# Taking A's last two wo rows out of the even DMA spread in a two-head decode kernel

## The chip, the cores and the metric

The kernel runs on one core of one Trainium2 chip. Times are device microseconds (us) of that core, one number for each execution; "median" is the median over the executions of one kernel.

In the trace of this kernel TensorE runs the matmuls (2148 of them), VectorE and ScalarE the elementwise work, copies and reductions (146 and 133 instructions), SyncE issues the large DMAs, and each of these has 16 landings, which are read here as those of 16 DMA engines. The program keeps the results of its matmuls in PSUM and places them by partition (row) and bank. The granted clock is the share of its full speed at which TensorE was allowed to run, as the clock's records of a profile give it; its mean over the span is 0.69 in the kernel before.

## The reference

Two attention decodes of one token, A and B, each end in a product with a [4096, 512] matrix `wo`. Only that last product matters here.

```python
def _A_ref(x, k_cache, v_cache, wq, wo):          # B is the same over the last 4096 keys
    q = (x @ wq).reshape(1, 1, 32, 128) ...       # 32 heads of 128
    scores = einsum("bhqd,bhkd->bhqk", q, k) * (128 ** -0.5)   # k, v: 16384 keys for A
    p = softmax(scores); o = einsum("bhqk,bhkd->bhqd", p, v)
    return o.reshape(1, 1, 4096) @ wo             # wo: [4096, 512], bf16, 4 MB
return concatenate([a, b], axis=-1)               # [1, 1, 1024]
```

## The kernel before

The kernel streams 352 MB, nearly all of it K and V, through one DMA queue, in program order, and loads the two `wo` matrices (4 MB each) at the end of the same queue. A `wo` row block of 32 rows lies on each of 128 partitions, so a product with `wo` is 32 matmuls of a one-column weight, 128 deep. A's piece is loaded as 16 and 16 rows a partition, B's as 16, 8, 4, 2 and 2.

```python
def _load_wo(nc, cx, st, j0, n):                       # one piece: n rows a partition
    ...
    src = st.wo.rearrange("(p j) f -> p j f", j=J)     # J = 32
    cx.o(nc.sync.dma_start(out=st.wo_t[:, j0:j0+n, :], in_=src[:, j0:j0+n, :]))

def _fin_rows(nc, cx, sts):                            # attention results -> columns
    for st in sts:                                     # sums of the softmax weights
        cx.o(nc.tensor.matmul(cx.f_ps[st.f_at:st.f_at+H, DH:DH+1], lhsT=cx.cs[:, st.f_at:st.f_at+H], ...))
    ...                                                # recip, orow, then 4 matmuls each into oc_ps

def _out(nc, cx, st, j0, n):                           # multiply one piece
    if j0 == 0:
        st.oc = ...; cx.o(nc.vector.tensor_copy(st.oc[:, :], st.oc_ps[:, 0:J]))
    if cx.out_ps is None:
        cx.out_ps = cx.red_pool.tile([P, 2, 512], F32, tag="red", name="out_ps")
    w = st.DN // st.cols
    out = [cx.out_ps[r:r+1, b, 0:w] for r, b in st.out_at]
    for j in range(j0, j0 + n):
        for x in range(st.cols):
            cx.o(nc.tensor.matmul(out[x], lhsT=st.oc[:, j:j+1], rhs=st.wo_t[:, j, x*w:(x+1)*w],
                                  start=(j == 0), stop=(j == J-1)))
    if j0 + n == J:
        row = ...; cx.o(nc.vector.tensor_copy(row[0:1, 0:w], out[0]))        # "rowA", "rowB"
        if st.cols == 2: cx.o(nc.scalar.copy(row[0:1, w:], out[1]))
        cx.o(nc.sync.dma_start(out=cx.out[...], in_=row[0:1, :]))

# st.out_at: (partition, PSUM bank) of the result
st.out_at = ((0, 0),) if name == "A" else ((64, 0), (96, 1))   # B in two halves of 256 columns
...
pieces = [(stA, 0, J//2), (stA, J//2, J//2)]           # loads, and later multiplications, in this order
j0 = 0
for x in (J//2, J//4, J//8, J//16, J//16):
    pieces.append((stB, j0, x)); j0 += x
...
_fin_rows(nc, cx, (stA, stB))
for p in pieces:
    _out(nc, cx, *p)
```

A's result and the first half of B's lie in the same PSUM bank, number 0, on different partitions.

The softmax here doesn't subtract the row's maximum and nothing guards it: scores larger than these inputs give would overflow.

## Time and profile before

| | before |
|---|---|
| time, median of the 3 runs first given | 823.26 us |
| traffic | 352.6 MB at 429 GB/s |
| busy: VectorE, TensorE | 73%, 37% |
| last B `wo` piece landed | 818.16 us |
| B's last matmul ended | 818.59 us |
| span of the profile | 821.2 us |

Times within a profile count from the first instruction. The first lines are the page of the kernel before: busy time by engine; the DMA engines' busy tenths in 40 slices of the span; the packets; and the queue that fetches instructions.

```profile
PE 301.1 (37%) x2148; PEld 117.3 (14%) x2148; DVE 600.7 (73%) x146; ACT 35.1 (4%) x133; POOL 1.3 (0%) x9
...
DMA  9999999999999999999999999999999999999997
...
DMA packets 8235, 352.62 MB, mean 429 GB/s; under 512 B 916, under 2 KB 920, under 8 KB 1304
...
q8 instruction: 16, 0.26, 0.1%
```

The DMA digit is 9 in every slice but the last: until the tail there is nothing to gain but bytes. The chain of waits of the kernel before (start, duration, what the span was waiting for) ends so:

```profile
756.43 32.55 DMA vt<-in_B_v_cache_dram
788.99 0.02 issue
789.00 29.16 DMA wo_t<-in_B_wo_dram
818.16 0.04 issue
818.21 0.43 PE out_ps L307 x4
818.63 0.41 DVE rowB L316
```

The last DMA engine to finish sets the end. After it come four matmuls, a copy and a store. The timeline of TensorE in the kernel before (start, duration, operation, and in brackets the idle time before it with what ended it):

```profile
803.73 8.75 PE L307 MATMUL out_ps<-wo_t,ocA 128*1 128x512 bf16 x32 [0.25 <-DVE ocA L300]
813.35 1.91 PE L307 MATMUL out_ps<-wo_t,ocB 128*1 128x256 bf16 x32 [0.87 <-DVE ocB L300]
815.69 1.04 PE L307 MATMUL out_ps<-wo_t,ocB 128*1 128x256 bf16 x16 [0.43 <-DMA wo_t<-in_B_wo_dram]
816.91 1.00 PE L307 MATMUL out_ps<-wo_t,ocB 128*1 128x256 bf16 x12 [0.18 <-DMA wo_t<-in_B_wo_dram]
818.21 0.38 PE L307 MATMUL out_ps<-wo_t,ocB 128*1 128x256 bf16 x4 [0.29 <-DMA wo_t<-in_B_wo_dram]
```

In B's phase TensorE waits for data three times, 0.9 us in all (0.43, 0.18 and 0.29). That is all the slack it has: delay it by more and TensorE sets the end, not the DMA.

The opportunity that the change aims at is in the per-engine completions. The trace has 16 updates of the semaphore of a DMA that is spread over all engines, each taken here as one engine's share landing. For the last B piece before, in us:

```
814.96 815.09 815.11 815.21 815.31 815.47 815.65 815.92 | 817.77 817.88 817.92 817.98 817.99 818.10 818.10 818.16
```

Eight engines are done 1.85 us or more before the other eight (815.92 to 817.77); first to last is 3.20 us. In the windows view of the kernel before, the last 5 us that matter (length; busy us of TensorE, its weight loads, VectorE, ScalarE, GpSimd; granted clock; DMA share; GB/s) have the DMA engines busy for 28%:

```profile
core 0: us, PE busy (x) PEld busy (x) DVE busy (x) ACT busy (x) POOL busy (x), PEclk, DMA share, GB/s
...
815.00:820.00 5.00, 2.67 (x38) 1.36 (x32) 0.42 (x1) 0.37 (x1) 0.00 (x0) 1.00 0.28 109
```

### The profile page before, as it was taken

The numbers are of one execution on the slowest core, as the hardware profiler recorded it, in microseconds if no ns is written. First come the engines' busy times: TensorE is split into PE (matmuls) and PEld (weight loads), VectorE is DVE, ScalarE is ACT, GpSimd is POOL, SyncE is SP. The second block draws the span as 40 slices with busy tenths as digits, with TensorE's granted clock in tenths as the row PEclk, the third lists the DMA queues.
The fourth block names the chain that finished last, engine by engine and source line by source line (L and its number), as shares of the span: only waits on it lengthen the run. The fifth ranks groups of instructions, "written<-read, shape, count | busy, mean of one in ns | idle before, by whom it ended". The sixth has DMA issues, their size and how long they took to land.

```text
span 821.2 us, 4767 instructions
## 1 busy us (share of the span) xinstructions
PE 301.1 (37%) x2148; PEld 117.3 (14%) x2148; DVE 600.7 (73%) x146; ACT 35.1 (4%) x133; POOL 1.3 (0%) x9
## 2 busy tenths in 40 slices
PE   3433705143223415060606151423414250606076
PEld 1111202011011102020202020101101020202033
DVE  2099895997496867799196949599659677689921
ACT  0100000000010000000001000000001000000010
POOL 0000000000000000000000000000000000000000
PEclk9855668586767677675858585857666676768599
DMA  9999999999999999999999999999999999999997
GB/s 383 434 457 412 456 412 454 412 454 418 427 442 444 425 441 429 441 416 447 421 445 437 431 435 434 432 423 443 441 418 451 425 445 421 448 413 455 413 424 317
DMA packets 8235, 352.62 MB, mean 429 GB/s; under 512 B 916, under 2 KB 920, under 8 KB 1304
## 3 DMA queue, kind: packets, MB, share of 16 engines
q1 hardware_dynamic: 8212, 352.33, 99.3%
q8 instruction: 16, 0.26, 0.1%
q14 instruction: 3, 0.02, 0.0%
q10 hardware_dynamic: 4, 0.00, 0.0%
HBM read 352.32 MB, written 0.00 MB: 429 GB/s over the span
## 4 chain that ended last, share of the span: by engine, by line
DMA 61%; issue 15%; DVE 13%; PE 11%; ACT 0%; SPq 0%; DVEq 0%
DMA kt<-in_A_k_cache_dram 42%; DMA vt<-in_A_v_cache_dram 12%; PE red L190 7%; DVE kt L178 6%; DVE kt L169 4%; PE acc L231 4%; DMA vt<-in_B_v_cache_dram 4%; DMA wo_t<-in_B_wo_dram 4%; DVE sc L206 2%; ACT p_sb L212 0%; SPq L115 0%; PE out_ps L307 0%; DVE rowB L316 0%; DVEq L169 0%
## 5 line engine op out<-in xcount | busy, mean ns | idle before, releaser
L169 DVE TENSOR_TENSOR kt<-kt,qallA 128x32768 bf16<-128x32768 bf16 (+2 forms) x20 | 276.2, 13810 | 162.5 <-DMA kt<-in_A_k_cache_dram 162.5
L231 PE MATMUL acc<-vt,p_sb 128*8 128x512 bf16 (+1 forms) x1280 | 113.0, 530 | 444.4 <-ACT p_sb L212 344.4
L178 DVE TENSOR_TENSOR kt<-kt 128x16384 bf16<-128x16384 bf16 (+2 forms) x24 | 174.3, 7261 | 0.2
L190 PE MATMUL red<-kt,ident 128*128 128x512 bf16 x640 | 151.2, 396 | 54.6 <-DVE kt L178 54.6
L231 PEld LDWEIGHTS <-p_sb 128*8 128x8 bf16 (+1 forms) x1280 | 37.6, 112 | 515.7 <-ACT p_sb L212 419.8
L190 PEld LDWEIGHTS <-ident 128*128 128x128 bf16 x640 | 63.0, 101 | 142.2 <-issue 47.1
L169 DVE TENSOR_TENSOR kt<-kt,qallB 128x16384 bf16<-128x16384 bf16 x8 | 69.5, 8686 | 2.9 <-DMA kt<-in_B_k_cache_dram 2.9
L206 DVE TENSOR_REDUCE sc<-red 128x256 f32<-128x2048 f32 x20 | 45.7, 2284 | 5.6 <-PE red L190 5.6
L212 ACT ACTIVATE p_sb<-sc,offA 128x256 bf16<-128x256 f32 x32 | 16.0, 500 | 574.7 <-DVE sc L206 574.7
L245 DVE TENSOR_TENSOR acc<-acc,maskA 128x512 f32<-128x512 f32 x16 | 11.1, 694 | 21.4 <-PE acc L231 21.4
L212 ACT ACTIVATE p_sb<-sc,offB 128x128 bf16<-128x128 f32 x32 | 12.4, 388 | 161.2 <-DVE sc L206 161.2
L130 PE MATMUL q_ps<-wq_t,scr 128*128 128x512 bf16 x64 | 15.7, 407 | 6.9 <-DMA wq_t<-in_A_wq_dram 4.9
L251 DVE TENSOR_REDUCE s<-acc 128x128 f32<-128x512 f32 x24 | 16.6, 691 | 0.8
L307 PE MATMUL out_ps<-wo_t,ocA 128*1 128x512 bf16 x32 | 8.8, 443 | 0.3 <-DVE ocA L300 0.3
L245 DVE TENSOR_TENSOR acc<-acc,maskB 128x512 f32<-128x512 f32 x8 | 5.5, 692 | 4.5 <-PE acc L231 4.5
L130 PEld LDWEIGHTS <-scr 128*128 128x128 bf16 x64 | 6.5, 103 | 15.6 <-issue 8.0
L316 DVE CAST rowA<-out_ps 1x512 bf16<-1x512 f32 x1 | 0.7, 678 | 8.8 <-PE out_ps L307 8.8
L259 PE MATMUL f_ps<-s,selA 128*32 128x128 f32 x32 | 6.5, 285 | 0.0
L212 ACT ACTIVATION_READ_ACCUMULATOR p_sb<-sc,offA 128x1 f32 x32 | 6.0, 187 | 0.0
L212 ACT ACTIVATION_READ_ACCUMULATOR p_sb<-sc,offB 128x1 f32 x32 | 6.0, 186 | 0.0
L307 PE MATMUL out_ps<-wo_t,ocB 128*1 128x256 bf16 x64 | 4.3, 272 | 1.8 <-DMA wo_t<-in_B_wo_dram 0.9
L102 DVE CAST scr<-xT 128x128 bf16<-128x128 f32 (+1 forms) x6 | 2.1, 459 | 3.6 <-PE xT L94 3.5
(43 smaller groups left out, 26.4 us busy)
## 6 DMA issues: line engine op xcount, KB each, us to landing
kt<-in_B_k_cache_dram SPq DMA_DIRECT2D x8, 4096.0 KB, 32.4
vt<-in_B_v_cache_dram SPq DMA_DIRECT2D x8, 4096.0 KB, 23.8
wq_t<-in_A_wq_dram SPq DMA_DIRECT2D x1, 4096.0 KB, 12.2
wq_t<-in_B_wq_dram SPq DMA_DIRECT2D x1, 4096.0 KB
wo_t<-in_A_wo_dram SPq DMA_DIRECT2D x2, 2048.0 KB, 22.6
wo_t<-in_B_wo_dram SPq DMA_DIRECT2D x1, 2048.0 KB, 27.0
wo_t<-in_B_wo_dram SPq DMA_DIRECT2D x1, 1024.0 KB, 29.0
wo_t<-in_B_wo_dram SPq DMA_DIRECT2D x1, 512.0 KB
```

Of the source, the lines that this page charges most:

```text
L102: cx.o(nc.vector.tensor_copy(st.xb[:, :, g, :].rearrange("p c (i r) -> p r c i", r=R)[:, g, :, :], xT[:, :].rearrange("p (c o) -> p c o", ...
L130: cx.o(nc.tensor.matmul(q_ps[:, j, :], lhsT=st.xb[:, c, g, :], rhs=w[:, g, j * (512 // DH) : (j + 1) * (512 // DH), :], start=(g == 0 and ...
L169: cx.o(nc.vector.tensor_tensor(out=k, in0=k, in1=q.rearrange("p (o d) -> p o d", o=1).broadcast_to([P, b - a, DH]), op=ALU.mult,))
L178: cx.o(nc.vector.tensor_tensor(out=k[:, :, 0 : DH // 2], in0=k[:, :, 0 : DH // 2], in1=k[:, :, DH // 2 : DH], op=ALU.add,))
L190: cx.o(nc.tensor.matmul(load.red[:, k : k + n, :], lhsT=cx.ident[:, :], rhs=load.kt[:, k : k + n, b * W : (b + 1) * W], start=(b == 0), st ...
L206: cx.o(nc.vector.tensor_reduce(out=sc[:, :], in_=load.red[:, :, :], axis=AX.X, op=ALU.add))
L212: cx.o(nc.scalar.activation(out=u.p[:, :, g, :], in_=sc[:, u.k0 : u.k0 + n].rearrange("p (t e) -> p t e", e=4), func=ACT.Exp, scale=SCALE, ...
L231: cx.o(nc.tensor.matmul(u.acc[r : r + 4 * R, :], lhsT=u.p[:, t, :, :], rhs=u.load.vt[:, k : k + 4, :], start=(t < 4), stop=(t >= T - 4),))
L245: cx.o(nc.vector.tensor_tensor(out=acc, in0=acc, in1=st.mask[:, :].rearrange("p (x o) -> p x o", o=1).broadcast_to([P, 4, DH]), op=ALU.mult,))
L251: cx.o(nc.vector.tensor_reduce(out=u.s[:, :], in_=acc.rearrange("p x d -> p d x"), axis=AX.X, op=ALU.add,))
L259: cx.o(nc.tensor.matmul(cx.f_ps[st.f_at : st.f_at + 32, 0:DH], lhsT=st.sel[:, at : at + 32], rhs=u.s[:, :], start=(u.i == 0), stop=(u.i == ...
L307: cx.o(nc.tensor.matmul(out[x], lhsT=st.oc[:, j : j + 1], rhs=st.wo_t[:, j, x * w : (x + 1) * w], start=(j == 0), stop=(j == J - 1),))
```

## The change

The intent: give bytes of the late engines to the early ones. A's last two rows of each partition (256 KB, 16 KB an engine) are no longer spread over 16 engines. They go into a tile of their own, `wo_x`, by eight DMAs whose slowest dimension is 5 or 3. They are meant to run on only 5 or 3 engines. Four of 5 blocks are queued behind A's `wo` and four of 3 blocks behind B's first 16 rows. Heads 0 to 19 land on partitions 0 to 19, heads 20 to 31 on 32 to 43, so these rows are multiplied 44 deep, by eight matmuls whose weights (`oc_x`) a small "spread" matmul puts in place. Along with it, the two sums of the softmax weights become one matmul, the copies `ocA` and `ocB` both come ahead of A's matmuls, and B's last piece of two rows is cut into two of one row.

```diff
+APART = 2
...
+def _load_apart(nc, cx, st, part):
+    J = st.wo.shape[0] // P
+    H = st.wo.shape[0] // DH
+    n = DH // J
+    if part == 0:
+        cx.wo_x = cx.kt_pool.tile([P, n, APART, st.DN], BF16, tag="kt", name="wo_x")
+        cx.o(nc.gpsimd.memset(cx.wo_x[0:32], 0.0))
+    src = st.wo.rearrange("(h r j) f -> h r j f", h=H, j=J)
+    h0, to, k = ((0, 0, 5), (20, 32, 3))[part]
+    for a in range(4):
+        cx.o(nc.sync.dma_start(
+            out=cx.wo_x[to + a : to + a + 4 * k - 3 : 4],
+            in_=src[h0 + a : h0 + a + 4 * k - 3 : 4, :, J - APART : J, :],
+        ))
...
-    for st in sts:
-        cx.o(nc.tensor.matmul(
-            cx.f_ps[st.f_at : st.f_at + H, DH : DH + 1],
-            lhsT=cx.cs[:, st.f_at : st.f_at + H], rhs=cx.ones_col[:, 0:1],
+    cx.o(nc.tensor.matmul(
+        cx.f_ps[0 : 2 * H, DH : DH + 1], lhsT=cx.cs[:, :], rhs=cx.ones_col[:, 0:1],
...
+    cx.out_ps = cx.red_pool.tile([P, 3, 512], F32, tag="red", name="out_ps")
...
+            cx.o(nc.tensor.matmul(moved, lhsT=cx.spread[:, :], rhs=orow[...][:, :, J - st.apart : J], ...))
+            st.oc_x = cx.small.tile([64, n * st.apart], BF16, tag="oc_x", name="oc_x")
+            cx.o(nc.vector.tensor_copy(st.oc_x[:, :], moved))
...
+        st.oc = cx.singles.tile([P, J], BF16, tag=f"oc{st.name}", name=f"oc{st.name}")
+        cx.o(nc.vector.tensor_copy(st.oc[:, :], st.oc_ps[:, 0:J]))
...
+    todo = [(st.oc[:, j : j + 1], st.wo_t[:, j, :]) for j in range(j0, j0 + n)]
+    last = j0 + n == J - st.apart
+    if st.apart and last:
+        todo += [
+            (st.oc_x[0:44, i : i + 1], cx.wo_x[0:44, i // st.apart, i % st.apart, :])
+            for i in range(DH // J * st.apart)
+        ]
...
-    pieces = [(stA, 0, J // 2), (stA, J // 2, J // 2)]
+    pieces = [(stA, 0, J // 2), (stA, J // 2, J // 2 - APART)]
-    for x in (J // 2, J // 4, J // 8, J // 16, J // 16):
+    for x in (J // 2, J // 4, J // 8, J // 16, J // 32, J // 32):
...
+        if i in (1, 2):
+            ld.add("kt" if i == 1 else None, lambda i=i: _load_apart(nc, cx, stA, i - 1))
```

More of the change, by code (lines that the diff above doesn't have):

```diff
@@ L268, in _fin_rows @@
     H = 32
-    for st in sts:
-        cx.o(nc.tensor.matmul(
-            cx.f_ps[st.f_at : st.f_at + H, DH : DH + 1],
-            lhsT=cx.cs[:, st.f_at : st.f_at + H], rhs=cx.ones_col[:, 0:1],
-            start=False, stop=True, skip_group_check=True,
-        ))
+    cx.o(nc.tensor.matmul(
+        cx.f_ps[0 : 2 * H, DH : DH + 1], lhsT=cx.cs[:, :], rhs=cx.ones_col[:, 0:1],
+        start=False, stop=True, skip_group_check=True,
+    ))
     recip = cx.small.tile([2 * H, 1], F32, tag="recip", name="recip")
@@ L284, in _fin_rows @@
         h = st.f_at
+        if st.apart:
+            moved = cx.out_ps[0:64, 2, 0 : n * st.apart]
+            cx.o(nc.tensor.matmul(
+                moved, lhsT=cx.spread[:, :],
+                rhs=orow[h : h + H, :].rearrange("p (r j) -> p r j", j=J)[:, :, J - st.apart : J],
+                start=True, stop=True, skip_group_check=True,
+            ))
+            st.oc_x = cx.small.tile([64, n * st.apart], BF16, tag="oc_x", name="oc_x")
+            cx.o(nc.vector.tensor_copy(st.oc_x[:, :], moved))
         for r in range(n):
@@ L293, in _fin_rows @@
             ))
+        st.oc = cx.singles.tile([P, J], BF16, tag=f"oc{st.name}", name=f"oc{st.name}")
+        cx.o(nc.vector.tensor_copy(st.oc[:, :], st.oc_ps[:, 0:J]))
 def _out(nc, cx, st, j0, n):
     J = st.wo.shape[0] // P
-    if j0 == 0:
-        st.oc = cx.singles.tile([P, J], BF16, tag=f"oc{st.name}", name=f"oc{st.name}")
-        cx.o(nc.vector.tensor_copy(st.oc[:, :], st.oc_ps[:, 0:J]))
-    if cx.out_ps is None:
-        cx.out_ps = cx.red_pool.tile([P, 2, 512], F32, tag="red", name="out_ps")
     w = st.DN // st.cols
     out = [cx.out_ps[r : r + 1, b, 0:w] for r, b in st.out_at]
-    for j in range(j0, j0 + n):
+    todo = [(st.oc[:, j : j + 1], st.wo_t[:, j, :]) for j in range(j0, j0 + n)]
[5 more added lines that the diff above has]
+        ]
+    for i, (oc, wo) in enumerate(todo):
         for x in range(st.cols):
             cx.o(nc.tensor.matmul(
-                out[x],
-                lhsT=st.oc[:, j : j + 1],
-                rhs=st.wo_t[:, j, x * w : (x + 1) * w],
-                start=(j == 0),
-                stop=(j == J - 1),
+                out[x], lhsT=oc, rhs=wo[:, x * w : (x + 1) * w],
+                start=(j0 == 0 and i == 0), stop=(last and i == len(todo) - 1),
             ))
-    if j0 + n == J:
+    if last:
         row = cx.accs_pool.tile([1, st.DN], BF16, tag="accs", name=f"row{st.name}")
@@ L375, in problem @@
         st.cols = len(st.out_at)
+        st.apart = APART if name == "A" else 0
         st.f_at = 0 if name == "A" else 32
@@ L444 @@
     )
+    cx.spread = cx.singles.tile([32, 64], BF16, tag="spread", name="spread")
+    nc.vector.memset(cx.spread[:, :], 0.0)
+    nc.vector.tensor_copy(cx.spread[:, 0:20], cx.ident[0:32, 0:20])
+    nc.vector.tensor_copy(cx.spread[:, 32:44], cx.ident[0:32, 20:32])
     cx.cs = cx.singles.tile([P, 64], F32, tag="cs", name="cs")
@@ L485 @@
     stB.oc_ps = cx.acc[1]
-    cx.out_ps = None
     _spread_x(nc, cx, stA, 0, 0)
```

## The prediction

> **What bounds it now.** The page gives 352.6 MB at 429 GB/s and a DMA digit of 9 in every slice but the last; VectorE is busy 73%, TensorE 37%. The chain of waits is 61% DMA, and its last 29.2 us are one wait for B's wo, up to 818.2 us; then 0.4 us of matmuls, a 0.4 us copy and the store, to 821.2. So the last DMA engine sets the end.
>
> The engines do not finish together. In the trace's semaphore increments, every late transfer lands in two groups of eight: the last one (256 KB) at 815.0 to 815.9 us on eight engines and at 817.8 to 818.1 on the others. The skew grows over the run: the queue table's 16 instruction packets of 16 KB each delay an engine by about 1.2 us, and eight engines get two each.
>
> **What the change does.** A's last two rows a partition (256 KB) leave the even spread: 16 KB less an engine. A 256 KB piece takes 0.61 us in the tail (2 KB packets of 80 ns), so each engine ends 0.6 us sooner. The same bytes return in DMAs whose outer dimension is 5 or 3. [...] B's last pieces of one row use 1 KB packets (46 ns, as for xrow): +0.1 us.
>
> Eight more issues of about 0.43 us wait for a GpSimd memset (estimated 3.5 us from the smaller memsets, done near 796) and for reused semaphores, some until A's wo lands (803.5 and 808.4); over 2 MB is queued then, so no late engine starves. TensorE: 38 matmuls of 512 columns for A instead of 32, +6 x 0.21 = 1.3 us, starting after the second wo_x group lands (about 812.2). It gets back the 0.9 us gap between A and B (both copies now come first). A ends near 813.6 and B's 3.9 us of matmuls near 817.7: the chain still ends on B's wo. The added setup hides behind the first K load (42 us).
>
> **Predicted: 822.6 us** (-0.65), range 821.8 to 824.3. Faster by over 2%: 0.3%; within 2%: 98.7%; slower by over 2%: 1%.
>
> **What would show it.** Last B landing at 817.5 instead of 818.1; spread of the last landings 1 us or less instead of 3.1; wo_x landings with 11 or 13 early increments and 5 or 3 late ones; B's last matmul right after its load; DMA share of 815 to 820 us above 0.28.
>
> **What would make it wrong.** [...] If wo_x's second group lands late, B's matmuls pile up behind it (+1 us). If small-k issues take longer, B's last pieces start late. A half-speed clock stretch (now 804.7 to 808.1) shifting onto B's matmuls costs 1 to 2 us.

The sum came to 822.6 us, 0.65 below the 823.26 first measured. Terms are cut from it where marked: which engines take the small DMAs, what these engines gain and where they end, and the risk that one of them is late. The 0.6 us that each engine ends sooner puts the late eight at 817.5.

Measured numbers, from the trace of the kernel before: the spread of a DMA's landings grows from 0.46 us for the first K load to 3.20 us; an instruction fetch took 0.88 to 1.0 us; the late eight land on average 2.65 us behind the early eight, which is 1.3 us for each of two fetches where the prediction has 1.2; successive 256 KB pieces land 0.62 to 0.67 us apart on an engine; a 2 KB packet took 84 ns, where the prediction has 80, and a 1 KB one 46. The GpSimd memset took 3.50 us in the trace after.

## The result, and the profile after

The changed kernel took 826.13 us (median of 825.23, 826.51, 826.94 and 825.75), against 823.44 of the kernel before in the same rounds. The ratio is 1.0032, 95% interval 1.0014 to 1.0049. A ratio in this document is the mean time of one kernel's runs over that of the other's of the same rounds, so not quite the ratio of the medians quoted. The prediction was 822.6 us with a range up to 824.3: wrong in sign, 3.5 us above the figure and 1.8 us above the range.

Run again later (c_after below), the same kernel scattered more. Its ten executions fall into three groups: three at 823.5 to 823.8, four at 825.2 to 826.9 and three at 828.3 to 829.1. The kernel before has no such groups. The profile shown here is of the run of 825.23 us.

The page after: the same traffic and 305 more packets, GpSimd's memset, and one instruction fetch more.

```profile
PE 303.5 (37%) x2153; PEld 118.3 (14%) x2153; DVE 601.0 (73%) x150; ACT 35.1 (4%) x133; POOL 4.8 (1%) x10
...
DMA packets 8540, 352.63 MB, mean 428 GB/s; under 512 B 964, under 2 KB 1224, under 8 KB 1608
...
q8 instruction: 17, 0.28, 0.1%
```

The chain of waits after has a different end. B's `wo` is no longer in it:

```profile
784.65 23.15 DMA wo_t<-in_A_wo_dram
...
808.56 4.08 DMA wo_x<-in_A_wo_dram
...
815.54 5.37 PE out_ps L337 x64
```

The timeline of TensorE after shows where the time went; three idle times and durations are to be compared with the five lines of before:

```profile
804.17 6.86 PE L337 MATMUL out_ps<-wo_t,ocA 128*1 128x512 bf16 x30 [0.27 <-DVE ocA L321]
812.88 1.88 PE L337 MATMUL out_ps<-wo_x,oc_x 44*1 44x512 bf16 x8 [1.85 <-DMA wo_x<-in_A_wo_dram]
815.54 5.32 PE L337 MATMUL out_ps<-wo_t,ocB 128*1 128x256 bf16 x64 [0.77 <-DVE rowA L343]
```

TensorE idles 1.85 us for the second group of `wo_x` DMAs, spends 1.88 us on the eight added matmuls, idles 0.77 us until the copy of A's row is done, and then needs 5.32 us for B's 64 matmuls without waiting once. It ends at 820.86, where before ended at 818.59: 2.27 us later, and the profiled runs differ by 2.02 us (825.23 and 823.21). The windows view after, same columns as above, gives the last piece of it:

```profile
815.00:820.00 5.00, 4.46 (x52) 3.03 (x53) 0.48 (x1) 0.00 (x0) 0.00 (x0) 0.66 0.42 155
```

The mean granted clock is 0.66: in the clock's records it was at half speed from 816.25 to 819.66 and at full speed around it, and (1.25 + 0.5 x 3.41 + 0.34) / 5 is 0.66. Before, this stretch of the span ran at 1.00. The clock's records of both kernels hold two states only, 0.5 and 1.0. The half-speed stretches in the tail are 3.41 us or 6.83 us (twice that) long in the profiles, and a 512-column matmul starts every 0.216 us at full speed and every 0.427 us at half. TensorE was not idle ahead of the stretch on B: in the 3.41 us before it (812.84 to 816.25) it was busy for 2.60 us. What those 2.60 us were made of is taken up under "Open" below.

The same window shows the DMA share at 0.42 instead of 0.28, so the engines do finish more evenly. The SyncE queue after (start, duration, issues) shows what the small DMAs cost it:

```profile
794.87 3.27 SPq L161 DMA_DIRECT2D wo_x<-in_A_wo_dram  x4
798.18 0.44 SPq L147 DMA_DIRECT2D wo_t<-in_B_wo_dram  x1
798.67 10.59 SPq L161 DMA_DIRECT2D wo_x<-in_A_wo_dram  x4
809.30 4.22 SPq L147 DMA_DIRECT2D wo_t<-in_B_wo_dram  x5
```

A `wo_x` issue takes 0.71 us (median), a `wo_t` one about 0.43; whether the few partitions or the access pattern cost it was not tested. Two of the second four wait for a semaphore to come free: they start at 803.38 and 807.82, and A's two `wo` pieces have landed at 803.36 and 807.80. B's first 16 rows (2 MB), issued at 798.18, were landing until 812.65, and the pieces behind them, issued from 809.30 on, landed in turn up to 818.26; so the landings show no hole from the slow issues.

The completions of the DMAs in question after, in us (the first number of a `wo_x` DMA is an update 0.4 us after the end of its issue, the others are read as the engines):

```
wo_x, 5 blocks, first : 796.18 | 804.98 805.17 805.35 805.50 805.85
wo_x, 3 blocks, last  : 809.68 | 812.13 812.32 812.64
B's last piece        : 816.62 816.66 816.71 816.88 816.97 817.16 817.31 817.35 817.36 817.41 817.43 817.45 817.46 817.59 817.65 818.26
```

Each `wo_x` DMA has one update early and then 5 or 3, where a DMA over all engines has 16; the size of the first is not in the trace, and 11 or 13 would make up 16. All five engines are early ones (A's piece just ahead has its early half at 804.63 to 805.53 and its late half at 807.42 to 807.80). So are the three: the first DMA of 3 blocks landed at 811.15 to 811.65, and the late half of B's first 16 rows, queued ahead of it, at 812.29 to 812.65. Fifteen engines now end within 1.03 us of each other, at 816.62 to 817.65, and one at 818.26.

### The profile page after: what moved, and what is told of

Same layout as the page of the kernel before. It is cut to its first block, busy times and chain, and to the rows that moved or that the text cites. A ratio compares the mean times of both kernels' runs of the same rounds, so it can differ in the third digit from the quotient of the medians. Undisturbed runs are those within 1.5% of the kernel's fastest.

```text
span 823.4 us, 4796 instructions
## 1 busy us (share of the span) xinstructions
PE 303.5 (37%) x2153; PEld 118.3 (14%) x2153; DVE 601.0 (73%) x150; ACT 35.1 (4%) x133; POOL 4.8 (1%) x10
## 4 chain that ended last, share of the span: by engine, by line
DMA 60%; issue 15%; PE 12%; DVE 12%; ACT 1%; SPq 0%; DVEq 0%
DMA kt<-in_A_k_cache_dram 41%; DMA vt<-in_A_v_cache_dram 15%; PE red L208 6%; PE acc L249 6%; DVE kt L196 5%; DVE kt L187 4%; DMA wo_t<-in_A_wo_dram 3%; DVE sc L224 2%; PE out_ps L337 1%; ACT p_sb L230 1%; DMA wo_x<-in_A_wo_dram 0%; SPq L116 0%; SPq L161 0%; DVE rowA L343 0%; DVE rowB L343 0%
## 5 line engine op out<-in xcount | busy, mean ns | idle before, releaser
L157 POOL MEMSET wo_x<- 32x4096 bf16 x1 | 3.5, 3501 | 789.4 <-PE red L208 789.4
L337 PE MATMUL out_ps<-wo_t,ocA 128*1 128x512 bf16 x30 | 6.8, 379 | 0.3 <-DVE ocA L321 0.3
```

The costliest lines, as they stand in the source:

```text
L157: cx.o(nc.gpsimd.memset(cx.wo_x[0:32], 0.0))
L337: cx.o(nc.tensor.matmul(out[x], lhsT=oc, rhs=wo[:, x * w : (x + 1) * w], start=(j0 == 0 and i == 0), stop=(last and i == len(todo) - 1),))
```

## The experiments

Every kernel ran in turn with the kernel before on the same chip. Edits are against the changed kernel unless said otherwise. "Added matmuls" write to a PSUM place whose result is not used; they leave the output right and only keep TensorE busy. The theory to be tested came from the profile: the DMA side works, and the loss is TensorE's, made of the wait for `wo_x`, the wait for the copy of A's row, and a half-speed clock stretch on B's matmuls. The rivals: the wait for the second `wo_x` group alone; late DMA engines; the merged sum of the softmax weights; noise between batches.

### c_after and c_before: both kernels again

No edit.

> The changed kernel again, unedited, as a base on the same chip as the three that follow. All theories: about 826 (825.2 to 826.9 in its four runs so far), ratio 1.003. By the clock theory single runs step between about 824 and 827 as one, or no, half-speed stretch falls on the last matmuls; by the DMA theory the runs lie within 1 us, as those of the kernel before do.

Measured: 826.05 us median (828.58, 823.47, 828.31, 823.76, 829.14, 823.79), ratio 1.0035 [1.0013, 1.0058]. The TensorE timeline of the run of 828.58 us:

```profile
806.90 9.50 PE L337 MATMUL out_ps<-wo_t,ocA 128*1 128x512 bf16 x30 [0.27 <-DVE ocA L321]
816.33 1.89 PE L337 MATMUL out_ps<-wo_x,oc_x 44*1 44x512 bf16 x8
818.99 5.33 PE L337 MATMUL out_ps<-wo_t,ocB 128*1 128x256 bf16 x64 [0.77 <-DVE rowA L343]
```

There is no wait for `wo_x` here at all. The clock was at half speed at 795.66 to 802.49, 805.90 to 812.73 and 819.56 to 822.97. It made A's 30 matmuls take 9.50 us instead of 6.86, and B's were hit again. The last B load landed at 818.07, before B's matmuls had begun. The stretch that ended at 802.49 came before A's rows, which started 2.73 us later than in the first profile (806.90 against 804.17). So the slow group is the same loss with more half-speed stretches, on A and just before it, and no story of DMA or of the wait for `wo_x` covers it.

> The kernel before, submitted as a kernel. 822.8 to 823.9 in every run, ratio 1.000. Its profile shows the half-speed stretches at another phase: by the theory B's matmuls still end within 0.6 us of the last load, because A's end by 814 whatever the phase.

Measured: 822.95 us (823.22, 822.89, 822.95, 823.77, 822.85), ratio 1.0001 [0.9988, 1.0013]. In its profile the clock was at half speed at 797.74 to 801.15 and 804.57 to 807.98, the second of these on A's matmuls:

```profile
805.03 8.51 PE L307 MATMUL out_ps<-wo_t,ocA 128*1 128x512 bf16 x32 [0.25 <-DVE ocA L300]
814.41 3.71 PE L307 MATMUL out_ps<-wo_t,ocB 128*1 128x256 bf16 x60 [0.87 <-DVE ocB L300]
818.37 0.38 PE L307 MATMUL out_ps<-wo_t,ocB 128*1 128x256 bf16 x4 [0.25 <-DMA wo_t<-in_B_wo_dram]
```

Even with this stretch, B's matmuls are done in time for the last load, with 0.25 us to spare. The kernel before absorbs what the changed one cannot.

### e16: all the DMAs, none of the added matmuls (wrong result)

```diff
-            for i in range(DH // J * st.apart)
+            for i in range(0)
```

> The changed kernel with all its DMAs, but without the eight wo_x matmuls (wrong result on purpose): the DMA share of the change alone. Theory: the last load lands at 817.5, B ends within 0.4 us of it where TensorE is not late: 822.3 to 822.8 in most runs, ratio 0.999, with at most some runs late. Rival (the small DMAs cost something themselves): 823.5 or more in every run.

Measured: 822.76 us (822.22, 822.76, 824.59, 822.26, 823.33), ratio 0.9998 [0.9985, 1.001]. In the profiled run (822.22) the last B load landed at 817.62, 0.54 us sooner than before, and B's matmuls ended at about 817.9. In its two best runs (822.22 and 822.26) the rebalanced DMA is worth 0.8 us, close to the 0.65 predicted; by the medians it is 0.27 us (822.76 against 823.03), and the ratio is 1 within the noise. So the DMA half of the prediction holds where TensorE is not late, and the added DMAs are ruled out as the cause of the loss. The run of 824.59 us has no profile; what delayed it is open.

### e8 and e19: the rest of the change without the moved rows

```diff
-        st.apart = APART if name == "A" else 0
+        st.apart = 0
-    pieces = [(stA, 0, J // 2), (stA, J // 2, J // 2 - APART)]
+    pieces = [(stA, 0, J // 2), (stA, J // 2, J // 2)]
-        if i in (1, 2):
-            ld.add("kt" if i == 1 else None, ...)
```

> Changed kernel without the moved rows: A's wo loaded in two even halves as before, no small DMAs and no wo_x; the other edits stay (both copies of oc before A's matmuls, one sum for the two row sums, B's last two loads of one row each). Clock theory: A ends near 811 to 812.5, B's matmuls wait for their loads as before, so a half-speed stretch is hidden: 823.0 to 823.5, ratio 1.000, runs within 1 us. If the other edits are what costs: 825 or more, or single runs at 828.

Measured: 823.25 us (824.98, 823.25, 822.85, 825.39, 823.08), ratio 1.0009 [0.9997, 1.0022]. The profile happens to be of the run of 824.98, in which the granted clock was 0.85 wherever it is otherwise 1.0 (0.85 at 816 to 820 us; 0.652 on average over the span), the only profile here with a third state.

> The changed kernel without the moved rows, again, for more samples (822.85 to 823.25 in three runs, 825.39 in one, and 824.98 in a profiled run at a clock of 0.85). If the edits ahead of A's matmuls make the runs unsteady by themselves: one or two of six at 825 to 828. If the moved rows are needed: 822.8 to 823.5 in all or all but one.

Measured: 822.95 us (822.7, 825.05, 823.24, 822.95, 822.81), ratio 1.0005 [0.9992, 1.0019]. Of ten runs, one is spoiled by its 0.85 clock, seven are at 822.7 to 823.3, and two, at 825.05 and 825.39, have no profile and stay unexplained. So the moved rows bring the loss in the main; the merged sum, the earlier copies and the smaller last pieces by themselves cost nothing in most runs.

### e18: the two sums apart again

```diff
-    cx.o(nc.tensor.matmul(cx.f_ps[0 : 2 * H, ...], lhsT=cx.cs[:, :], ...))
+    for st in sts:
+        cx.o(nc.tensor.matmul(cx.f_ps[st.f_at : st.f_at + H, ...], lhsT=cx.cs[:, st.f_at : st.f_at + H], ...))
```

> The changed kernel with the two separate row-sum matmuls of the kernel before in place of the merged one. If the merged sum (less TensorE activity ahead of A's matmuls) brings the two half-speed windows on A: 825 at most in every run, no run at 828. If what matters is the work that the change put after the load of B's first rows: as the changed kernel, runs between 823.5 and 829, ratio 1.003.

Measured: 825.1 us (825.1, 823.59, 825.03, 825.31, 826.65), ratio 1.0025 [1.0012, 1.0038]. The clock was at half speed from 815.35 to 818.76, and B's matmuls took 5.14 us. The loss is there as before: the merged sum is not its cause.

### e2: no wait for the second group (wrong result)

```diff
-            (st.oc_x[0:44, i : i + 1], cx.wo_x[0:44, i // st.apart, i % st.apart, :])
+            (st.oc_x[0:20, i : i + 1], cx.wo_x[0:20, i // st.apart, i % st.apart, :])
```

> Changed kernel with all DMAs as they are, but A's wo_x matmuls contract rows 0 to 19 alone, so TensorE does not wait for the second group of wo_x (wrong result on purpose). Theory (the place of the second group, behind B's first 16 rows, costs the time): no 1.9 us gap before the wo_x matmuls, A ends near 812.8, B starts near 813.5, no half-speed stretch on B's matmuls, B ends right after its last load (817.5): 822.4 to 822.8, ratio 0.999. Rival (DMA queue sets the end): no change, ratio 1.003.

Measured: 826.4 us (824.53, 824.53, 828.48, 828.77, 823.7, 828.26), ratio 1.0038 [1.0019, 1.0058]. A plain miss, and a useful one. The 1.85 us wait is gone from the profile, yet the clock was at half speed on A (804.69 to 808.10, A's matmuls took 8.32 us) and again on B (814.93 to 818.34, 5.30 us), and the 0.77 us wait for the copy is still there. The wait for the second group alone is not what costs the time. The probe is not quite clean, as it also makes the `wo_x` matmuls 20 instead of 44 deep, which may itself favour a half-speed stretch (see "Open"); but c_after above, whose profile has no such wait either, says the same.

### e4: four DMAs of 8 blocks, all behind A's wo

```diff
-    h0, to, k = ((0, 0, 5), (20, 32, 3))[part]
+    h0, to, k = 0, 0, 8
...                                        # and 0:32 for 0:44, all four after A's second piece
```

> Changed kernel with the 32 blocks in four DMAs of 8 blocks, all queued behind A's wo, on partitions 0 to 31, contracted 32 deep. [...] the wo_x landings come before 808 us, so A's 38 matmuls run without a gap. Theory: 822.3 to 822.8 (ratio 0.999), faster than both. [...] If eight DMAs or four makes no difference and the DMA queue is what costs, ratio 1.001 to 1.003.

Measured: 823.52 us (823.82, 823.52, 823.51, 823.48, 823.94), ratio 1.0005 [0.9993, 1.0017]. The first of these DMAs had eight engine increments, six at 804.82 to 805.67 and two at 807.76 and 807.88: six of these engines are early and two are late. The two late ones then carry extra bytes, and the last B load lands at 818.74. Two outcomes are cut from the expectation, because they went by the numbers of the engines, which no trace of this case shows. Here everything of `wo_x` is there in time, TensorE goes from A's rows to `wo_x` without a pause, B runs at full speed (3.66 us) in the profile, and the five runs lie within 0.5 us.

### e1: B's result in other PSUM banks

```diff
-        st.out_at = ((0, 0),) if name == "A" else ((64, 0), (96, 1))
+        st.out_at = ((0, 0),) if name == "A" else ((64, 1), (96, 2))
```

> Changed kernel, with B's two output rows in PSUM banks 1 and 2, so that B's first matmul no longer waits for the copy of A's row out of bank 0 (0.77 us in the changed kernel's trace). Theory (TensorE's tail is the critical path): B's matmuls start 0.7 to 0.8 us sooner and the kernel is 0.7 us faster than the changed one (about 825.4, ratio to before 1.0023). Rival (the DMA queue, slowed by eight small issues, sets the end): no change, 826.1, ratio 1.003.

Measured: 823.84 us (822.75, 825.97, 824.46, 823.01, 826.02, 823.22), ratio 1.0012 [0.9999, 1.0025]. In the profiled run (822.75) the wait for the copy is gone and B runs at full speed:

```profile
813.01 1.88 PE L337 MATMUL out_ps<-wo_x,oc_x 44*1 44x512 bf16 x8 [0.15 <-issue]
814.83 3.66 PE L337 MATMUL out_ps<-wo_t,ocB 128*1 128x256 bf16 x64
```

So the 0.77 us are due to the shared bank: nothing else was changed. The gain was larger than expected (2.2 us by the medians, against c_after of another batch, instead of 0.7), but not steady: two runs are still at 826. The bank takes away a fixed cost and, in the profiled run, the half-speed stretch on B as well; two runs without a profile did not keep that gain.

### e6: eight added matmuls ahead of wo_x

```diff
+        if st.apart and last and i == n:
+            for _ in range(8):
+                cx.o(nc.tensor.matmul(cx.out_ps[64:65, 2, 0:w], lhsT=st.oc[:, 0:1], rhs=st.wo_t[:, 0, :], ...))
```

> Changed kernel with eight added matmuls of 512 columns into an unused bank while TensorE waits for the second wo_x group (their results are not used; the output is right). Theory (of the 2.7 us, up to 1.8 us is a half-speed clock stretch on B's matmuls that follows the gap): the clock stays 1.0, B's 64 matmuls take 3.4 us instead of 5.3, and it is 1.5 us faster than the changed kernel, 824.4 (ratio 1.001). If the half-speed stretch has nothing to do with the gap: no change or slower, ratio 1.003 or more.

Measured: 823.81 us (825.38, 823.81, 823.47, 823.3, 825.46), ratio 1.0009 [0.9996, 1.0022]. Inconclusive. In its profile (825.38) the added matmuls, which write to partition 64 where A's write to partition 0, started together with A's last ones (810.21 and 810.22, 810.43 and 810.43), so a gap of 1.23 us stayed, and a half-speed stretch at 816.28 to 819.70 came on B (5.33 us). The probe did not do what it was made for. The next one sends the added matmuls to partition 0; there they ran after A's (A's 14 from 808.41, the 11 added ones from 811.43).

### e9: TensorE kept busy from the last attention block on

```diff
+def _warm(nc, cx, k):
+    for _ in range(k):
+        cx.o(nc.tensor.matmul(cx.warm_ps[0:1, :], lhsT=cx.ident[:, 0:1], rhs=cx.warm_in[:, 0:512], ...))
...
+    if st.cols == 2 and j0 == 0: _warm(nc, cx, 3)                # before B
+        if st.apart and last and i == n: _warm(nc, cx, 11)       # before wo_x
+    _warm(nc, cx, 12)                                            # before the last p @ v
+        _warm(nc, cx, 4)                                         # before each of its two folds
```

> Changed kernel with added matmuls (results unused, output right) in every gap of TensorE from the last softmax on: 12 before the last P times V, 4 before each last fold, 11 before wo_x, 3 before B. Clock theory: no half-speed stretch after about 790 us, A's 30 matmuls take 6.5 us and B's 64 take 3.4 to 3.7 us, B ends near 819.0 (still behind the wo_x group that lands at 812.7 and the copy of A's row), 823.6 to 824.0, ratio 1.0005 to 1.001, and the runs lie within 1 us of each other. If the clock is not the cause: 826, and the spread stays 2 us or more.

Measured: 824.16 us (824.49, 823.88, 824.16, 824.23, 824.03), ratio 1.0011 [0.9999, 1.0023]. The clock was at 1.0 from 782.4 to 823.4, and the five runs lie within 0.61 us where the changed kernel's lie within 5.7:

```profile
813.90 1.88 PE L349 MATMUL out_ps<-wo_x,oc_x 44*1 44x512 bf16 x8
816.55 3.66 PE L349 MATMUL out_ps<-wo_t,ocB 128*1 128x256 bf16 x64
```

B takes 3.66 us instead of 5.32, the difference of 1.66 us being the clock's. This is 1.89 us below c_after's median, although `wo_x` starts 1.02 us later than in the first profile (813.90 against 812.88): its load lands 0.43 us later here (813.07 against 812.64), and the added matmuls are not done when it lands. Holding the clock removes the scatter and most of the loss.

### e10: e9 with the banks apart

Against e9:

```diff
-    if st.cols == 2 and j0 == 0: _warm(nc, cx, 3)
-        st.out_at = ((0, 0),) if name == "A" else ((64, 0), (96, 1))
+        st.out_at = ((0, 0),) if name == "A" else ((64, 1), (96, 2))
```

> The last one without the 3 matmuls before B, and with B's output rows in banks 1 and 2, so that B does not wait for the copy of A's row. Theory (clock and copy are two separate parts of the loss): B's matmuls start at 814.8 and end near 818.4, as in the profiled run of the bank-only kernel, 822.8 to 823.1, ratio 0.9995, stable within 1 us. Rival (the bank edit helps only through the clock): same as the last one, 823.6 to 824.0.

Measured: 823.17 us (823.06, 823.25, 823.17, 823.36, 823.0), ratio 0.9999 [0.9986, 1.0012], as expected.

```profile
813.30 1.89 PE L347 MATMUL out_ps<-wo_x,oc_x 44*1 44x512 bf16 x8
815.12 3.66 PE L347 MATMUL out_ps<-wo_t,ocB 128*1 128x256 bf16 x64
```

B now starts as `wo_x` ends, and is done at 818.78, still 0.65 us after the last load (818.13). That the 3 matmuls are gone is not the gain: in e9 the copy of A's row ended at 816.50, and B started at 816.55. The two edits take the whole loss away in steps, 826.05 to 824.16 to 823.17, and leave the time of the kernel before. TensorE is still the last by a little: `wo_x` starts at 813.30 where the prediction needed its end by 813.6.

### e11 and e13: A's rows in two halves of columns

e11, against e10: A's result also in two halves of 256 columns on two partition groups, four banks, 6 added matmuls before A's second piece and 8 instead of 11 before `wo_x`.

```diff
-        st.out_at = ((0, 0),) if name == "A" else ((64, 1), (96, 2))
+        st.out_at = ((0, 0), (32, 1)) if name == "A" else ((64, 2), (96, 3))
+    if not st.f_at and j0: _warm(nc, cx, 6)
-            _warm(nc, cx, 11)
+            _warm(nc, cx, 8)
```

> As the last one, but A's wo also goes through two column groups (256 columns each, four banks in all), which halves the time of A's and of wo_x's matmuls, with 6 added matmuls before A's second half and 8 before wo_x. Theory (what holds the end above the last load of 817.5 is TensorE's 5.5 us of work after the second wo_x group lands at 812.7): that work is 4.4 us, B ends 0.2 to 0.4 us after the last load, near 817.8, and the kernel takes 822.2 to 822.6, ratio 0.999: the size that was predicted for the change. If the DMA queue ends it in any case: 823 or more.

Measured: 823.69 us (823.69, 823.73, 824.68, 823.36, 823.49), ratio 1.0006 [0.9994, 1.0018]. A miss. The `wo_x` matmuls now take 1.03 us (1.88 in the first profile), but the added ones were too few, and the clock went to half at 814.93:

```profile
813.07 1.03 PE L349 MATMUL out_ps<-wo_x,oc_x 44*1 44x256 bf16 x16 [1.91 <-DMA wo_x<-in_A_wo_dram]
814.04 5.32 PE L349 MATMUL out_ps<-wo_t,ocB 128*1 128x256 bf16 x64
```

e13, against e11, changes one number:

```diff
-            _warm(nc, cx, 8)
+            _warm(nc, cx, 15)
```

> The two-column-group kernel with 15 added matmuls before wo_x instead of 8, so that the 1.9 us gap is filled, after which B's matmuls ran at half speed in its profile. Clock theory: B's matmuls at full speed, B ends near 817.8 right after its last load (817.5): 822.1 to 822.5, ratio 0.999, faster than both. If the half speed does not come from the gap: 823.7 again.

Measured: 823.4 us (823.35 to 823.47), ratio 1.0003 [0.9991, 1.0016].

```profile
812.93 1.03 PE L349 MATMUL out_ps<-wo_x,oc_x 44*1 44x256 bf16 x16
813.94 1.91 PE L349 MATMUL out_ps<-wo_t,ocB 128*1 128x256 bf16 x32
816.22 1.04 PE L349 MATMUL out_ps<-wo_t,ocB 128*1 128x256 bf16 x16 [0.37 <-DMA wo_t<-in_B_wo_dram]
...
817.45 1.53 PE L349 MATMUL out_ps<-wo_t,ocB 128*1 128x256 bf16 x16 [0.19 <-DMA wo_t<-in_B_wo_dram]
```

This pair is the cleanest test of the clock. With seven more matmuls in the gap, the gap and the half-speed stretch are both gone, and B waits for its loads again, as it did before the change. The time is still 823.4, not the 822.1 to 822.5 expected: one engine's last load lands at 818.66, the others' by 817.79. (In e11 too one engine was late, at 818.87 with the others done by 817.85, but B ended after it, at 819.36.)

### e14: e10 without the second group and without the 11 (wrong result)

```diff
-            (st.oc_x[0:44, ...], cx.wo_x[0:44, ...])
+            (st.oc_x[0:20, ...], cx.wo_x[0:20, ...])
-            _warm(nc, cx, 11)
```

> The kernel with added matmuls and separate banks, but wo_x contracted over rows 0 to 19 alone, so that it does not wait for the second group (wrong result on purpose), and without the 11 matmuls before wo_x. Theory (with clock and copy out of the way, the second group's place in the queue costs what is left): A ends near 812.8, B waits for its loads, ends near 817.8: 822.2 to 822.6, 0.6 to 0.9 us below the same kernel with the wait (823.17). If the second group's place costs nothing: 823.2.

Measured: 823.51 us (823.45 to 823.68), ratio 1.0005 [0.9992, 1.0018]. TensorE is done with `wo_x` at 812.8 and waits 1.42 us ahead of B's last four matmuls, for one engine that lands at 819.0 while the others are done by 817.69. The miss is the same as in e13: with TensorE out of the way, one straggling engine takes the gain.

### e12 and e15: added work in the kernel before

e12 puts the 12 and 4 + 4 added matmuls of e9 into the kernel before; e15 puts 6 ahead of its last A matmul.

```diff
+    _warm(nc, cx, 12)                             # e12: before the last p @ v
+        _warm(nc, cx, 4)                          # e12: before each fold
...
+        for i in range(6 if st.cols == 1 and j == J - 1 else 0):          # e15
+            cx.o(nc.tensor.matmul(cx.out_ps[64:65, 1, 0:w], ...))
```

> The kernel before with the same added matmuls before the last P times V and the last folds. Theory (the kernel before ends on its last load, TensorE has slack): no change, 823.0 to 823.4, ratio 0.9995 to 1.0005. If the added matmuls by themselves are worth anything, or cost anything, it shows here.

Measured: 824.29 us (824.53, 824.17, 824.29, 823.29, 824.53), ratio 1.0011 [0.9998, 1.0025]: 1.1 us slower where nothing was expected. TensorE is not the reason:

```profile
819.73 0.38 PE L315 MATMUL out_ps<-wo_t,ocB 128*1 128x256 bf16 x4 [1.70 <-DMA wo_t<-in_B_wo_dram]
```

Its last four matmuls wait 1.70 us for one engine, which lands at 819.68 while the other fifteen are done by 818.23. A 17th instruction fetch of 16 KB started at 817.5 and took 0.97 us. The kernel before has this fetch too, but later: at 821.88 in c_before, after its work is done, and not within the first profile. The trace does not say which engine carries a fetch, so that the straggler is the one is inferred from the times, and was not shown. The fetches of e11, e13 and e14 that precede their stragglers came at 816.5, 811.9 and 816.8. It does not always cost: in e1, e16 and e17 the fetch came at 817.1 to 817.4 and no engine landed over 0.1 us after the rest.

> The kernel before with six extra matmuls of 512 columns (results unused) ahead of A's last one: TensorE's extra work of the change, without its DMAs. Theory (TensorE's tail has about 1 us to spare before the last load, and past that half-speed stretches show): the runs spread, some near 823.3, some at 824.5 to 828, mean ratio 1.001 to 1.004. Rival (the small DMAs or the wait for them are needed for the loss): 823.0 to 823.9 in every run, ratio 1.000.

Measured: 823.11 us (823.09 to 823.32), ratio 1.0 [0.9987, 1.0012]. Inconclusive: as in e6 the six, on partition 64, ran beside A's own matmuls (811.27 and 811.27, 811.70 and 811.70; A's row was complete at 812.56), so they did not delay TensorE, and the run says nothing of its slack.

### e17: B's first rows ahead of wo_x, with the banks apart

```diff
     for p in pieces:
-        _out(nc, cx, *p)
+        ...          # A's own rows, B's first 16 rows, then the wo_x matmuls, then B's rest
+                     # added matmuls: 6, 4 and 4, and 7 before B
```

> The changed kernel with B's first 16 rows multiplied ahead of wo_x, B's output rows in banks 1 and 2, and 21 added matmuls in TensorE's gaps (6 before the last P times V, 4 before each last fold, 7 before B). Theory: from the landing of B's first rows (812.45) TensorE has 5.2 us of work, so B ends near 817.9: 822.2 to 822.8, steady, faster than both, unless the seventeenth instruction fetch delays one engine's last load, as in the kernels with 31 and more added matmuls (one engine 0.4 to 1.4 us after the others): then 823.0 to 823.6.

Measured: 823.54 us (822.74, 823.54, 823.07, 823.8, 823.75), ratio 1.0004 [0.999, 1.0018]. The best run has what the order was meant to give (last load at 817.74, B done at about 818.3), but the others do not hold it, and they have no profile. No version with a right result beats the kernel before; e10 equals it.

## Why the prediction was wrong

**The DMA side was right.** Predicted: 5 or 3 late increments for a `wo_x` DMA, the late eight ending near 817.5 instead of 818.1, spread of the last landings 1 us or less, DMA share above 0.28. Measured: 5 and 3, all on engines of the early half by their times; fifteen engines at 816.62 to 817.65 and one at 818.26, so a spread of 1.64 us with it and 1.03 without; share 0.42. In e16, where TensorE does not stand in the way, the last load lands at 817.62, and the profiled run, the best of five, is 0.8 us under the median of the kernel before in its rounds (822.22 against 823.03).

**The failed step** is the prediction's "A ends near 813.6 and B's 3.9 us of matmuls near 817.7: the chain still ends on B's wo." Measured in the first profile: A ends at 814.76 and B at 820.86, and the chain ends on TensorE. The 3.16 us between 817.7 and 820.86 are three terms:

1. A's end, 1.16 us (814.76 less 813.6). Of this, 0.44 us is the load (812.64 instead of 812.2), 0.24 us the start after it (812.88), and 0.48 us the work: the eight matmuls take 1.88 us where 1.4 was allowed (812.2 to 813.6). The prediction counted six matmuls of extra work, when eight stand behind the wait.
2. The gap between A and B, 0.78 us (814.76 to 815.54). "It gets back the 0.9 us gap between A and B (both copies now come first)" was a misreading of the line `[0.87 <-DVE ocB L300]`. The profile names the releaser that came last. Behind `ocB` stood the copy of A's row out of bank 0, into which B's first half writes, and with `ocB` out of the way it holds TensorE for 0.77 us. e1 and e10 show it: with B in other banks the wait is gone.
3. The clock, 1.22 us (5.32 us against the 4.1 between 813.6 and 817.7). Half speed on B was listed as a risk of 1 to 2 us, not put into the sum. At full speed B takes 3.66 us (e9, e10), so the stretch costs 1.66. It was not chance alone that put it there: by the reading under "Open", the eight `wo_x` matmuls and the gaps beside them bring it on.

**The three groups of runs** then fit, as a reading. With B at full speed from 815.54 it ends at 819.2, 0.6 us after before's 818.59; the fast group is 823.5 to 823.8. With a half-speed stretch on B, 2.3 us later; the middle group is 825.2 to 826.9. With one on A as well, and one just before A (the profile of 828.58 us), the slow group. Only the middle and slow groups have a profile each.

**The loss and its undoing.** Holding the clock (e9) takes the median from 826.05 to 824.16, the banks (e10) take it to 823.17. Of the 0.65 us gain promised none is left at that point, since in e10 TensorE still starts `wo_x` at 813.30 and B still ends after its last load. The versions that got TensorE out of the way (e13, e14) met the straggling engine instead, and the two causes were not separated by a run that avoids both.

**Rivals.** The wait for the second group alone is refuted by e2 and by the profile of c_after; late engines as the cause of the loss by e16 and by the landings (818.26 and 818.07 in the two profiles of the changed kernel, 2.6 and 6.2 us before TensorE is done); the merged sum by e18; noise by c_after and c_before.

**Open.** What decides whether a half-speed stretch comes was tested by no run made for it, but the kept traces fit one reading. In the traces of the kernels before and after every whole stretch of the clock is a multiple of 3.413 us, to 1 ns, so the span is cut here into windows of that length. Take as a window's activity the share of it in which matmuls ran by the profile, and count a matmul that contracts r rows at r/128 of its time. In the 20 profiles a full-speed window under 0.40 was followed by half speed each time (445 windows) and one over 0.53 never (1205 windows; 149 lie between). A half-speed window over 0.77 was followed by full speed each time (461) and one under 0.76 never (2443). The traces of the first two profiles alone, before and after, have 44, 112, 47 and 245 such windows, without an exception.

The rows matter where `wo_x` is. Just before the stretch on B, TensorE was busy for 2.60 us of the window in the first profile and 2.65 in c_after, no less than in two windows of the kernel before at this place (2.54 from 811.53 to 814.94 and 2.49 from there to 818.35), which were followed by full speed. But 1.88 us of it were matmuls 44 deep. That makes the activity 0.40 and 0.43, against 0.75 and 0.73; in e2, e6, e11 and e18, which also had the stretch on B, it was 0.33 to 0.41. Where the gaps next to `wo_x` were closed it was 0.59 (e1) and 0.65 (e9, e10), and B kept full speed. So the change seems to bring the stretch on itself, by shallow matmuls with a gap beside them, and the kernel before, which has none among A's and B's rows, is spared. A gap of 1.9 us does not decide it alone.

What a fetch costs the loads beside it is read from the landings of the whole run of the kernel before. It has 16 fetches of 16 KB, 0.88 to 1.0 us each. Each of the first eight is followed by one more engine that lands 1.5 to 2.0 us behind the first to land, and each of the next eight by one of these that drops to about 3 us behind, so that in the end eight engines are late by two fetches each. A 17th within the tail went with one straggling engine, 0.9 to 1.5 us after the rest, in e11, e12, e13 and e14, but with none in e1, e16 and e17. Which engine carries a fetch is inferred from the times.

Not settled are the two smaller stragglers: in the first profile after the change and in e10 one engine was 0.6 and 0.4 us behind from B's second piece on, before the 17th fetch. The slow runs of e1, e8, e16 and e19 that have no profile are open too.

## What to carry to other kernels

When a transfer sets the end of a kernel, find out how far behind it the next engine is before making the transfer shorter: here TensorE had 0.3 to 0.9 us of slack, and the change put 1.9 us of dependent matmuls behind a late load. Take a wait's named releaser as the last of several, and look for what would hold the instruction next, such as the copy out of the same PSUM bank, 0.77 us here. A clock that was seen at half speed belongs in the sum of the expected time as a term with its cost (1.66 us on B here), above all in short tails where TensorE has gaps or, by the reading above, matmuls over few rows.
